# Reordering the expert tiles of a routed feed-forward kernel: five first tiles from the half lists, three experts from the full lists

## The chip, the core and the metric

The kernel runs on one core of a Trainium2 chip. A core has a matmul engine (PE, with its weight loads shown apart as PEld), a vector engine (DVE), a scalar engine (ACT), a general engine (POOL) and a queue engine (SP) that issues DMA transfers; POOL and ACT issue some as well. Each engine works through its own instructions in the order in which they were written, and waits on semaphores for the others. The metric is the device time of one execution in microseconds (us): 1375.17 us before the change, the median of three runs (1374.98 to 1376.15).

## The reference

Two stages. First a causal seven-tap convolution per head, with softmaxed taps (x is 8 x 3584 x 192, so 28,672 tokens of 192 numbers). Then a mixture of eight experts, where tokens are assigned to experts greedily by score under a capacity:

```python
logits = x @ w_gate                       # 28672 x 8
for idx in np.argsort(-logits.flatten()): # best score first
    tok, e = idx // 8, idx % 8
    if assigned[tok] >= 0 or counts[e] >= 3584: continue
    assigned[tok] = e; counts[e] += 1
for e in range(8):
    h = np.maximum(x[assigned == e] @ w1[e], 0.0)   # 192 -> 1024
    out[assigned == e] = h @ w2[e]                  # 1024 -> 192
```

Every expert ends with exactly 3584 tokens, which are seven tiles of 512.

## The kernel before, in words

**Stages.** The convolution runs as matmuls over sixteen blocks and writes its result to a DRAM scratch tensor `attn`; its transposes give the logits on the way. The feed-forward part (class `FFN`) then works through 56 tiles of 512 tokens (eight experts, tiles 0 to 6 each). For a tile the tokens are gathered from `attn` by an index list (POOL, L1206), transposed, multiplied by the first matrix (`l1`, tile `ph`), passed through ReLU, multiplied by the second (`l2`, tile `y`), and scattered to the output by the same list (POOL, L1274). Numbers are kept to full precision by splitting each into a high part and a low part: ACT writes `hh`, the high part of the hidden layer, and DVE writes `hl`, the rest. `run` interleaves, in eight steps f = 0 to 7, the first matrix of tile i with the second matrix of tile i - 1. At the top of tile i it issues the gather of tile i + 2, so the list of tile i + 2 has to be there by then.

**The lists.** Which tokens belong to which expert is worked out while the tiles run. This background work (`Steps`, class `Route`) is a chain of generators: `half(0)` makes lists `ia0` from the first half of the tokens, enough for tile 0 of every expert; `half(1)` makes the full lists `ia` for tiles 0 to 2 (tokens above a safe threshold); `rest` settles the remaining tokens in seven rounds and makes `ib0` (tile 3 of experts 0 to 2); `last` makes `ib` (the remaining tiles). A hook between matmuls takes a few steps of it whenever a planner's running sum says that DVE and ACT are not too far ahead of PE. Where a list is needed and not finished, `drain` writes the remaining steps down at once, with no tile work between them.

**The weights.** The matrices of an expert are also split into high and low parts. The first time an expert comes up, its weights arrive as eight raw pieces (SP, `raw`, four buffers); for each piece `wsplit` lets ACT write the high part and POOL (or DVE, for the two 64-row pieces) the low part (L1187, `w<-raw,w`), has SP store both parts to DRAM scratch (`kw`, `kd`, `kv`; L1190 to L1196), and only then has `wload` issue the raw load of the fourth piece ahead. When the expert comes up again, the split weights are fetched from the scratch in three transfers (`w<-kw`, `dl<-kd`, `w<-kv`), with no splitting. `plan` gives each piece the tile from which it may be handled: four pieces a tile, the first matrix while the tile before the expert's first is running, the second one tile later.

**The order before.** Tile 0 of experts 0 to 7 (tiles numbered 0 to 7 of the run), then tiles 1 and 2 of experts 7 down to 0 (run tiles 8 to 23), then tile 3 of experts 0 to 2, tiles 4 to 6 of experts 2 to 0, and tiles 3 to 6 of experts 3 to 7. So during run tiles 0 to 7 every tile splits eight raw pieces, and all of run tiles 8 to 21 fetch weights that were split before.

Of the kernel before, what the change touches and what calls it, by code (L numbers as in the profile page):

```python
# [10 lines left out]
OP = mybir.AluOpType  # L11
AX = mybir.AxisListType
PSUM = bass.MemoryType.PSUM

NE, D, NTOK, F, CAP = 8, 192, 28672, 1024, 3584
# [278 lines left out]
class Route:  # L294
# [307 lines left out]
    def counts(self, n0):  # L602


        nc, cst, wk = self.nc, self.cst, self.wk
        V, PE = nc.vector, nc.tensor
        n = wk.tile([128, 1], F32, name="k_n")
        self.set = cst.tile([128, 2], F32, name="set")
        V.tensor_scalar(wk.tile([128, G], BF, name="k_b"), self.M1, self.Ts, None, op0=OP.is_ge, op1=OP.add, accum_out=n)
        yield PEW  # L610
        ps = self.bg()
        PE.matmul(ps[:, 24:24 + n0], self.ones, self.tot[0][:, 0:n0], start=True, stop=True, skip_group_check=True)
        for h in range(2):
            PE.matmul(ps[:, 0:8], self.ones, self.tot[h], start=(h == 0), stop=(h == 1), skip_group_check=True)
        for h in range(2):
            PE.matmul(ps[0:8, 8:9], self.tot[h], self.ones[:, 0:1], start=(h == 0), stop=(h == 1), skip_group_check=True)
        PE.matmul(ps[:, 16:17], self.onesf, n, start=True, stop=True, skip_group_check=True)
        self.room = cst.tile([128, 8], F32, name="room")
        self.room8 = cst.tile([8, 1], F32, name="room8")
        b = wk.tile([128, 3], F32, name="k_c")  # L620
        V.tensor_scalar(self.room, ps[:, 0:8], -1.0, float(CAP), op0=OP.mult, op1=OP.add)
        V.tensor_scalar(self.room8, ps[0:8, 8:9], -1.0, float(CAP), op0=OP.mult, op1=OP.add)
        V.tensor_reduce(self.set[:, 1:2], ps[:, 0:8], axis=AX.X, op=OP.add)
        V.tensor_copy(self.set[:, 0:1], ps[:, 16:17])
        V.tensor_reduce(b[:, 2:3], ps[:, 24:24 + n0], axis=AX.X, op=OP.min)
        yield

        V.tensor_reduce(b[:, 0:1], self.room, axis=AX.X, op=OP.max)
        V.tensor_tensor(b[:, 1:2], self.set[:, 0:1], self.set[:, 1:2], op=OP.not_equal)
        V.tensor_scalar(b[:, 2:3], b[:, 2:3], 512.0, None, op0=OP.is_lt)  # L630
        V.tensor_scalar(b[:, 0:1], b[:, 0:1], float(CAP - 128 * TA), None, op0=OP.is_gt)
        V.tensor_reduce(self.bad, b, axis=AX.X, op=OP.max)
        yield
# [451 lines left out]
class FFN:  # L1085
# [47 lines left out]

    def wload(self):
        nc = self.nc
        if self.loaded == len(self.pieces) or self.pieces[self.loaded][3] in ("W1", "W2"):
            return
        _, (e, _), _, what, q = self.pieces[self.loaded]
        t = self.wr.tile([128, 512], F32, name="raw")
        s = slice(512 * q, 512 * q + 512)  # L1140
        if what == "a":
            nc.sync.dma_start(t, self.w1[e, 0:128, s])
        elif what == "d":
            nc.sync.dma_start(t[0:64], self.w1[e, 128:192, s])
            nc.sync.dma_start(t[64:128], self.w1[e, 128:192, s])
        else:
            nc.sync.dma_start(t[:, 0:2 * D].rearrange("p (k d) -> p k d", d=D),
                              self.w2[e, 256 * q:256 * q + 256].rearrange("(k p) d -> p k d", p=128))
        self.RAW[self.loaded] = t
        self.loaded += 1  # L1150
# [198 lines left out]
NL = 3  # L1349


def moe_kernel(ctx, tc, x, weight, wg, w1, w2, out):
    nc = Pace(tc.nc)
    V, P = nc.vector, nc.gpsimd
# [4 lines left out]
    with ExitStack() as cw:  # L1359
# [8 lines left out]
        r = Route(tc, nc, LT, lst, wk, drm)  # L1368
# [5 lines left out]
        ib = lst.tile([128, 8, TB], I32, name="ib")  # L1374
        ib0 = lst.tile([128, NL, 4], I32, name="ib0")

        order = [(e, (0,)) for e in range(NE)]
        order += [(e, (1, 2)) for e in range(NE - 1, -1, -1)]
        order += [(e, (3,)) for e in range(NL)]
        order += [(e, (4, 5, 6)) for e in range(NL - 1, -1, -1)]  # L1380
        order += [(e, (3, 4, 5, 6)) for e in range(NL, NE)]
# [6 lines left out]
        def half(h):  # L1388
            if h == 0:
                yield from r.thresh(0.905)  # L1390
            yield from r.settle(h)
            yield from r.count(r.F, h)
            if h:
                yield from r.counts(NE)
            yield from r.lists(r.F, TA, h, 0 if h else None, *((ia,) if h else (ia0, 8, 4)))

        def rest():
# [47 lines left out]
            k.logits_t(i)  # L1445
            r.top(i)

        def first(e):
            ff.gather(e, [ia0[:, e, b:b + 1] for b in range(4)], NTOK // 2, V)

        def gather():
            if ff.xg and not ff.XG:
# [74 lines left out]

        def idx_of(tile_):
            e, t = tile_[1]
            if t == 0:  # L1530
                return [ia0[:, e, b:b + 1] for b in range(4)]
            if t < 3:
                if len(bg.gens) > 2:
                    bg.drain(2)
                return [ia[:, e, 4 * t + b:4 * t + b + 1] for b in range(4)]
            if t == 3 and e < NL:
                if len(bg.gens) > 1:
                    bg.drain(1)
                return [ib0[:, e, b:b + 1] for b in range(4)]
            if bg.gens:  # L1540
                bg.drain()
            return [ib[:, e, 4 * (t - 3) + b:4 * (t - 3) + b + 1] for b in range(4)]
# [46 lines left out]
```

## Time and profile before

| | |
|---|---|
| median of three runs | 1375.17 us |
| the profiled execution | 1377.14 us, of which the span of its instructions is 1375.2 us |
| mean granted PE clock | 0.964 of full speed |
| first feed-forward matmul | 206 us after the span's start |
| DMA moved | 188.23 MB, 137 GB/s on average |
| weight fetches from scratch | 16 of 1536 KB (first matrix), 16 of 1536 KB (second), 16 of 256 KB |

The profile is one execution. Its page gives the busy time of each engine and the chain of work that ended last; other views of the same trace give each engine's instructions in order of time (with the idle time before an instruction and who ended it), groups of instructions by line and tile, and the busy time of every engine in chosen stretches. A stretch named "run tile 5" here reaches from the first `ph` matmul of that tile to the first of the next; each tile has 40 of them. The PE column of a stretch may be high while PE waits inside its pipeline, so the length of a stretch says more than its busy share.

### The profile page before, as it was taken

Reading aid. Unit: us, or ns where it says so; the run is one execution under the profiler, and the core shown is the slowest. Engines: PE = TensorE matmul, PEld = TensorE weight load, DVE = VectorE, ACT = ScalarE, POOL = GpSimd, SP = SyncE. Lnnn points to the kernel's source line nnn. Section 1 sums busy time; section 2 is a strip of 40 time slices with the busy share of each in tenths; the row PEclk is TensorE's granted clock in tenths of the full one; section 3 lists DMA queues with packets and bytes.
Section 4 is the critical chain, followed back from the end, with each engine's and each line's share of the span. In section 5 each row is a group of like instructions: output and inputs, shape, how many; then the busy total and the mean of one; then the engine's idle time right before and its main releaser. Section 6 shows DMA issues by size and latency. Waiting matters only on the chain.

```text
span 1375.2 us, 20862 instructions
## 1 busy us (share of the span) xinstructions
PE 1288.4 (94%) x7367; PEld 1106.8 (80%) x7367; DVE 1046.1 (76%) x2216; ACT 586.0 (43%) x1242; POOL 637.0 (46%) x607
## 2 busy tenths in 40 slices
PE   5978897998989999999959999999999999999997
PEld 2545564887879989889848999999999999999997
DVE  7598963777988888888877477777777777777772
ACT  4755473447544434434413433333333333333332
POOL 5655566556754443443403344444444444444432
PEclk9998897999999999999959999999999999999999
DMA  9996568677872443343312152324231414141110
GB/s 231 284 271 166 170 218 286 204 231 248 260 260 83 143 137 97 138 143 118 100 60 81 32 197 89 101 89 139 86 99 49 140 44 146 45 142 42 42 35 28
DMA packets 114431, 188.23 MB, mean 137 GB/s; under 512 B 12352, under 2 KB 86544, under 8 KB 110096
## 3 DMA queue, kind: packets, MB, share of 16 engines
q1 hardware_dynamic: 63888, 120.75, 27.6%
q0 software_dynamic: 21504, 44.07, 10.3%
q10 hardware_dynamic: 28928, 22.02, 4.9%
q8 instruction: 59, 0.97, 0.3%
q14 instruction: 52, 0.43, 0.1%
HBM read 114.44 MB, written 72.35 MB: 136 GB/s over the span
## 4 chain that ended last, share of the span: by engine, by line
PE 74%; DVE 14%; DMA 4%; issue 3%; ACT 2%; POOL 2%; SPq 0%; POOLq 0%; DVEq 0%; ACTq 0%
PE ph L53 34%; PE y L53 32%; PE bg L53 4%; DVE X L53 4%; DMA attn<-a 2%; DVE oa L53 2%; DVE aT L53 2%; PE cv L53 1%; DVE hl L53 1%; DMA raw<-in_moe_w_dram 1%; POOL xg L1206 1%; PE pl L53 1%; DVE TH L53 1%; PE pd L53 1%; ACT hi L53 1%
## 5 line engine op out<-in xcount | busy, mean ns | idle before, releaser
L53 PE MATMUL y<-w,hh 128*128 128x384 f32 x1792 | 541.7, 358 | 0.0
L53 ACT ACTIVATE hh<-ph 128x512 fp32r<-128x512 f32 x448 | 267.7, 598 | 508.7 <-PE ph L53 377.6
L53 DVE SCALAR_TENSOR_TENSOR hl<-ph,hh 128x512 fp32r<-128x512 f32 x448 | 308.5, 689 | 196.6 <-ACT hh L53 163.7
L53 PE MATMUL y<-w,hl 128*128 128x192 f32 x1792 | 450.3, 251 | 0.0
L53 PE MATMUL ph<-xa,w 128*128 128x512 f32 x1344 | 401.7, 407 | 17.3 <-DVE hl L53 13.3
L53 PEld LDWEIGHTS y<-w,hl 128*128 128x128 f32 x1792 | 342.8, 191 | 15.4
L53 PEld LDWEIGHTS y<-w,hh 128*128 128x128 f32 x1792 | 338.4, 189 | 17.1
L1274 POOL DMA_INDIRECT out_dram<-yo,ib x128 | 126.9, 992 | 294.9 <-DVE yo L53 279.5
L53 PEld LDWEIGHTS ph<-xa,w 128*128 128x128 f32 x1344 | 221.4, 191 | 42.2 <-DVE hl L53 16.4
L1274 POOL DMA_INDIRECT out_dram<-yo,ia x96 | 107.4, 1118 | 240.6 <-DVE yo L53 202.6
L53 DVE STREAM_TRANSPOSE xs<-xg 32x256 f32<-32x256 f32 x480 | 176.9, 369 | 8.3
L53 PE MATMUL ph<-xd,w 128*128 128x512 f32 x448 | 179.2, 400 | 0.0
L53 PE MATMUL ph<-xd,dl 128*128 128x512 f32 x448 | 176.0, 393 | 0.0
L1206 POOL DMA_INDIRECT xg<-attn,ib x128 | 130.1, 1016 | 70.2 <-issue 69.9
L226 POOL TENSOR_TENSOR lo<-aT,hi 128x768 fp32r<-128x768 f32 x50 | 93.3, 1896 | 73.5 <-ACT hi L53 73.5
L53 PE MATMUL cv<-X,TH 118*128 118x384 f32 x256 | 106.6, 548 | 19.2 <-DVE TH L53 12.8
L1206 POOL DMA_INDIRECT xg<-attn,ia x96 | 105.2, 1096 | 28.8 <-issue 27.6
L53 ACT ACTIVATE yt<-y 128x192 f32<-128x192 f32 x224 | 73.4, 328 | 97.5 <-PE y L53 87.5
L53 DVE TENSOR_TENSOR yo<-y,yt 128x192 f32<-128x192 f32 x224 | 79.6, 355 | 45.6 <-ACT yt L53 42.4
L53 PEld LDWEIGHTS cv<-X,TH 118*128 118x128 f32 x256 | 50.4, 210 | 65.2 <-issue 14.8
L53 PEld LDWEIGHTS ph<-xd,w 128*128 128x128 f32 x448 | 85.2, 190 | 21.3 <-issue 2.2
L53 PEld LDWEIGHTS ph<-xd,dl 128*128 128x128 f32 x448 | 85.1, 190 | 19.9 <-POOL dl L1187 0.3
(241 smaller groups left out, 1233.5 us busy)
## 6 DMA issues: line engine op xcount, KB each, us to landing
w<-kw SPq DMA_DIRECT2D x16, 1536.0 KB
w<-kv SPq DMA_DIRECT2D x16, 1536.0 KB
X<-in_x_dram SPq DMA_DIRECT2D x16, 1344.0 KB
attn<-a ACTq DMA_DIRECT2D x16, 1344.0 KB
kw<-w SPq DMA_DIRECT2D x48, 256.0 KB
kv<-w SPq DMA_DIRECT2D x32, 384.0 KB
raw<-in_moe_w_dram SPq DMA_DIRECT2D x32, 192.0 KB
raw<-in_moe_w_dram SPq DMA_DIRECT2D x16, 256.0 KB
```

Of the source, the lines that this page charges most:

```text
L53: return f(*a, **k)
L226: eng.tensor_tensor(lo, aT, hi.bitcast(F32), op=OP.subtract)
L1206: self.nc.gpsimd.indirect_dma_start(out=t[:, b], out_offset=None, in_=self.attn[0:rows], in_offset=bass.IndirectOffsetOnAxis(ap=idx[b], ax ...
L1274: st = nc.gpsimd.indirect_dma_start(out=self.out, out_offset=bass.IndirectOffsetOnAxis(ap=idx, axis=0), in_=o, in_offset=None, bounds_chec ...
```

## The change

The order of the tiles is written anew. Run tiles 0 to 4 are tile 0 of experts 7, 6, 5, 4 and 3, from the half lists. Then come tiles 1 and 2 of experts 3, 4, 5, 6, 7 (run tiles 5 to 14), and then tiles 0, 1, 2 of experts 2, 1 and 0 (run tiles 15 to 23), all from the full lists. From run tile 24 on the order of tiles is as before. The raw pieces of experts 2, 1 and 0 so come up at run tiles 13 to 19, behind four fetches from the scratch; `wload` now steps over fetches to find the next raw piece. The weights are fetched from scratch 13 times in place of 16. The check that the half lists are long enough looks at experts 3 to 7 alone.

```diff
-        PE.matmul(ps[:, 24:24 + n0], self.ones, self.tot[0][:, 0:n0], ...)
+        PE.matmul(ps[:, 24:32 - n0], self.ones, self.tot[0][:, n0:8], ...)
...
     def wload(self):
         nc = self.nc
-        if self.loaded == len(self.pieces) or self.pieces[self.loaded][3] in ("W1", "W2"):
+        while self.loaded < len(self.pieces) and self.pieces[self.loaded][3] in ("W1", "W2"):
+            self.loaded += 1
+        if self.loaded == len(self.pieces):
             return
...
-        order = [(e, (0,)) for e in range(NE)]
-        order += [(e, (1, 2)) for e in range(NE - 1, -1, -1)]
+        order = [(e, (0,)) for e in range(NE - 1, NL - 1, -1)]
+        order += [(e, (1, 2)) for e in range(NL, NE)]
+        order += [(e, (0, 1, 2)) for e in range(NL - 1, -1, -1)]
         order += [(e, (3,)) for e in range(NL)]
...
-                yield from r.counts(NE)
+                yield from r.counts(NL)
...
-            if t == 0:
+            if t == 0 and e >= NL:
                 return [ia0[:, e, b:b + 1] for b in range(4)]
             if t < 3:
                 if len(bg.gens) > 2:
                     bg.drain(2)
```

(`NE` is 8 and `NL` is 3.) The first run tile from the full lists is now number 5 in place of 8, so its gather stands at the top of run tile 3 in place of 6, and the last steps of `half(1)` are drained there. At the top of run tile 22 the drain that finishes `ib0` stands in both kernels.

**DVE at the top of run tile 3** (`oa` is a one-hot block of the list sort, `asm` the sorted list, `m_f` to `ia` the arithmetic that makes token numbers of it, `hl` and `yo` tile work). Before:

```order
L53 TENSOR_TENSOR oa<-irep,q 128x1024
L53 TENSOR_TENSOR dl<-raw,w_2604 64x512
L53 SCALAR_TENSOR_TENSOR hl<-ph,hh 128x512 x2
L53 TENSOR_TENSOR yo<-y,yt 128x192
L53 SCALAR_TENSOR_TENSOR hl<-ph,hh 128x512
L53 TENSOR_TENSOR asm<-asm,bg 128x192
L53 TENSOR_SCALAR m_f<-asm 128x96
```

With the change:

```order
L53 TENSOR_TENSOR oa<-irep,q 128x1024
L53 TENSOR_TENSOR dl<-raw,w_2604 64x512
L53 TENSOR_TENSOR asm<-asm,bg 128x192
L53 TENSOR_SCALAR m_f<-asm 128x96
L53 TENSOR_SCALAR off<-bad 128x1
```

The three `hl` of run tile 3 that lay between the sort and the list now come after the list.

**POOL in run tiles 4 and 5, and in 13 and 14** (`w<-raw,w` are the low parts of a raw piece, `xg` a gather, `out_dram` a scatter). Before, from the gather at the top of run tile 4 on, and so on to run tile 7:

```order
L1206 DMA xg<-attn,ia_105 128x192 x4
L1187 TENSOR_TENSOR w_3138<-raw,w_3138 128x2x192
L1274 DMA out_dram<-yo,ia_105 28672x192
L1187 TENSOR_TENSOR w_3138<-raw,w_3138 128x2x192 x2
L1274 DMA out_dram<-yo,ia_105 28672x192
L1187 TENSOR_TENSOR w_3138<-raw,w_3138 128x2x192
L1187 TENSOR_TENSOR w_3267<-raw,w_3267 128x512
L1274 DMA out_dram<-yo,ia_105 28672x192
L1187 TENSOR_TENSOR w_3267<-raw,w_3267 128x512
L1274 DMA out_dram<-yo,ia_105 28672x192
```

With the change the last split of the first phase stands in run tile 4; from run tile 13 on:

```order
L1208 DMA xg<-attn,ia 128x192 x4
L1189 TENSOR_TENSOR w_5319<-raw,w_5319 128x512
L1276 DMA out_dram<-yo,ia 28672x192
L1189 TENSOR_TENSOR w_5319<-raw,w_5319 128x512
L1276 DMA out_dram<-yo,ia 28672x192 x3
L1208 DMA xg<-attn,ia 128x192 x4
L1189 TENSOR_TENSOR w_5572<-raw,w_5572 128x2x192
L1276 DMA out_dram<-yo,ia 28672x192
L1189 TENSOR_TENSOR w_5572<-raw,w_5572 128x2x192 x2
L1276 DMA out_dram<-yo,ia 28672x192
L1189 TENSOR_TENSOR w_5572<-raw,w_5572 128x2x192
L1276 DMA out_dram<-yo,ia 28672x192 x2
```

The second half of run tile 4 and run tiles 5 to 7 lose 18 splits in all; run tiles 13 to 16, 18 and 19 get 2 or 4 each, 20 in all (for expert 0 POOL also takes the two 64-row pieces).

**DVE before the drain at run tile 22** (`X` and `c_mu` are the last pass over the scores, `F` the final assignment that the count on PE needs). Before, `F` is written in the drain, with no `hl` behind it:

```order
L53 TENSOR_TENSOR X_7539<-X_7423,c_mu 128x512
L53 TENSOR_TENSOR yo<-y,yt 128x192
L53 TENSOR_TENSOR X_7539<-X_7423,c_mu 128x512
L53 TENSOR_TENSOR X_7539<-X_7424,c_mu 128x512 x2
L53 SCALAR_TENSOR_TENSOR F<-X_7539,F 128x1024 x2
L53 TENSOR_SCALAR k_b,u_c<-c_mu 128x256
```

With the change:

```order
L53 SCALAR_TENSOR_TENSOR hl<-ph,hh 128x512
L53 SCALAR_TENSOR_TENSOR F<-X_7406,F 128x1024
L53 TENSOR_TENSOR yo<-y,yt 128x192
L53 SCALAR_TENSOR_TENSOR F<-X_7406,F 128x1024
L53 SCALAR_TENSOR_TENSOR hl<-ph,hh 128x512
L53 TENSOR_TENSOR xa<-pa,xa 128x512
L53 SCALAR_TENSOR_TENSOR hl<-ph,hh 128x512
```

`F` is now written inside run tile 21, with `hl` of that tile behind it.

More of the change, by code (lines that the diff above doesn't have):

```diff
@@ L611, in counts @@
         ps = self.bg()
-        PE.matmul(ps[:, 24:24 + n0], self.ones, self.tot[0][:, 0:n0], start=True, stop=True, skip_group_check=True)
+        PE.matmul(ps[:, 24:32 - n0], self.ones, self.tot[0][:, n0:8], start=True, stop=True, skip_group_check=True)
         for h in range(2):
@@ L624, in counts @@
         V.tensor_copy(self.set[:, 0:1], ps[:, 16:17])
-        V.tensor_reduce(b[:, 2:3], ps[:, 24:24 + n0], axis=AX.X, op=OP.min)
+        V.tensor_reduce(b[:, 2:3], ps[:, 24:32 - n0], axis=AX.X, op=OP.min)
         yield
@@ L1446, in end, with first @@
             r.top(i)
-        def first(e):
-            ff.gather(e, [ia0[:, e, b:b + 1] for b in range(4)], NTOK // 2, V)
+        def first(i):
+            e = tiles[i][1][0]
+            ff.gather(i, [ia0[:, e, b:b + 1] for b in range(4)], NTOK // 2, V)
         def gather():
```

## The prediction

> **What bounds the kernel now.** I read the page first, for the engine that carries the chain that ended last.
>
> ```profile
> PE 1288.4 (94%) x7367; PEld 1106.8 (80%) x7367; DVE 1046.1 (76%) x2216; ACT 586.0 (43%) x1242; POOL 637.0 (46%) x607
> PE 74%; DVE 14%; DMA 4%; issue 3%; ACT 2%; POOL 2%; SPq 0%; POOLq 0%; DVEq 0%; ACTq 0%
> ```
>
> PE is the bound, but a quarter of the chain is others' work. To see where, I cut the feed-forward part into stretches, one a run tile where the change acts. Columns: stretch, length, busy us (and instructions) of PE, PEld, DVE, ACT, POOL, then the granted clock, the DMA share and GB/s.
>
> ```profile
> 292.90:318.30 25.40, 22.62 (x163) 20.03 (x162) 17.69 (x34) 13.23 (x25) 14.29 (x13) 1.00 0.57 184
> 318.30:340.20 21.90, 19.99 (x115) 17.52 (x114) 12.03 (x19) 19.22 (x54) 15.14 (x15) 1.00 0.80 258
> 340.20:363.30 23.10, 20.45 (x114) 18.19 (x113) 22.79 (x36) 12.86 (x30) 16.70 (x16) 0.96 0.90 296
> 363.30:383.30 20.00, 20.00 (x115) 18.07 (x114) 17.45 (x39) 11.28 (x28) 14.70 (x14) 0.96 0.77 239
> 383.30:410.50 27.20, 22.58 (x121) 19.55 (x119) 23.60 (x56) 10.38 (x21) 13.57 (x13) 0.87 0.74 263
> 410.50:668.40 257.90, 256.85 (x1512) 230.68 (x1511) 220.10 (x522) 113.04 (x278) 113.72 (x104) 1.00 0.36 120
> 668.40:720.60 52.20, 37.48 (x325) 32.89 (x324) 41.55 (x107) 12.48 (x24) 9.39 (x9) 0.73 0.25 83
> 772.10:1340.20 568.10, 568.10 (x3235) 515.64 (x3234) 425.63 (x915) 215.52 (x434) 244.85 (x244) 1.00 0.27 91
> ```
>
> The first five rows are run tiles 3 to 7, the sixth is tiles 8 to 20 (13 of them, 257.9/13 = 19.84 each), the seventh tile 21 with the drain behind it, the last tiles 24 to 54 (31, 18.33 each). A tile alone costs 18.3; with rounds of background work beside it 19.8, PE never idle for more than 1.05 in 13 tiles, though every second tile fetches split weights there: fetches cost nothing, at a DMA share of 0.36. But tiles 4 to 7, which split raw pieces beside the same rounds, cost 21.9 + 23.1 + 20.0 + 27.2 = 92.2.
>
> Why: two causes. The first is in the chain of waits of tile 4 (start us, us, what).
>
> ```profile
> 331.11 1.03 POOL w L1187
> 332.16 0.32 SPq L1190
> ...
> 334.40 4.30 DMA raw<-in_moe_w_dram
> 338.72 0.55 ACT w L53
> 339.27 0.58 ACT hh L53
> ```
>
> A raw load is issued only after POOL's split and the store behind it; ACT waits for it, with `hh` queued behind, and PE waits for that. The second is in the order of time of DVE, POOL and PE in tiles 5 and 7, with one undisturbed row of tile 8:
>
> ```profile
> 350.83 2.71 DVE L53 SCALAR_TENSOR_TENSOR c_mu<-X 128x256 f32<-128x256 f32 x1
> 351.25 2.00 POOL L1187 TENSOR_TENSOR w<-raw,w 128x384 fp32r<-128x384 f32 x2
> 394.47 2.74 DVE L53 TENSOR_SCALAR r_dd<-r_d 128x8 f32<-128x8 f32 x1
> 395.19 1.98 POOL L1187 TENSOR_TENSOR w<-raw,w 128x384 fp32r<-128x384 f32 x2
> 360.12 0.96 PE L53 MATMUL ph<-xa,w 128*128 128x512 f32 x3 [1.79 <-DVE hl L53]
> 399.70 1.65 PE L53 MATMUL ph<-xa,w 128*128 128x512 f32 x3 [3.01 <-DVE hl L53]
> 424.27 0.41 DVE L53 SCALAR_TENSOR_TENSOR c_mu<-X 128x256 f32<-128x256 f32 x1
> ```
>
> While POOL does a pair of splits, a DVE instruction of 0.41 takes 2.71: it ends when the pair ends. `hl` is late, `ph` is not freed, PE idles 1.79 and 3.01, and behind it the clock drops (0.96 and 0.87 in those stretches).
>
> **The change part by part.** *A: run tiles 4 to 7 lose their splits.* They should cost what tiles 8 to 20 do: 4 x 19.84 = 79.4, so 12.8 less. Tile 4 keeps the four pieces of expert 3, but the late load in its chain is a piece of the next expert and goes. I take -12; bounds -9 (tile 4 keeps its 21.9 and tile 7 two of its 7.4 too many) and -13.
>
> *B: the drain at the top of run tile 3.* The rows for it are the same end of a list in the drain at tile 22 (chain of waits), and, in the order of time of PE and POOL and in the chain of waits, where the pieces stand now in tile 3:
>
> ```profile
> 715.41 0.61 ACT X L53
> 716.02 0.05 issue
> 716.06 1.09 PE bg L53 x8
> 717.17 1.95 ACT X L53 x2
> 719.12 0.04 issue
> 719.17 1.68 PE bg L53 x17
> 294.66 1.15 PE L53 MATMUL bg<-X,oa 128*128 128x16 bf16 x16
> 298.01 1.22 PE L53 MATMUL bg<-identb,X 128*128 128x128 bf16 x16
> 295.63 1.04 POOL L1206 DMA_INDIRECT xg<-attn,ia  x1 [0.30 <-issue]
> 304.49 1.03 POOL w L1187
> 305.54 0.32 SPq L1190
> 305.91 2.71 DMA raw<-in_moe_w_dram
> ```
>
> The last 16 sort matmuls (1.15), ACT's copy (0.61), half the transposes (1.22/2), two copies (1.95) and the last matmuls (of the 1.68 some 0.4 belong to the list) follow each other with nothing beside them: 1.15 + 0.61 + 0.61 + 1.95 + 0.4, with the small gaps about 5 us. Of it some 3 (1.15 + 1.22 + 0.7) is PE work that tile 3 does anyway, so 2 is new. Behind it: 13 small DVE instructions make the list, and `hl` of f = 0 waits for them; POOL's gather for tile 5, at 295.63 now, waits for the list (the drain's 5 and some 2.5 for the 13, counted from 292.9), about 5 later, and behind it stand the scatter of tile 2, four splits, the stores on SP and the raw loads that ACT waits for: the last three rows are on the chain, with no slack. PE is 2 later itself, so up to 3 more can surface; and a clock window can be lost:
>
> ```profile
> 360.00:365.00 5.00, 4.88 (x17) 4.36 (x18) 4.94 (x7) 1.97 (x6) 2.47 (x2) 0.66 0.95 297
> ```
>
> 0.34 of 5 us, 1.7, after an idle spell of 1.79. I take +4; bounds +2 (the drain alone) and +8 (2 + 3 and the clock lost twice).
>
> *C: the splits of experts 2, 1 and 0 in run tiles 13 to 16, 18 and 19.* Nothing is removed here: POOL does 20 splits in place of 18, at the mean of this group (all of the run):
>
> ```profile
> L1187 POOL TENSOR_TENSOR w<-raw,w 128x384 fp32r<-128x384 f32 (+1 forms) x48 | 52.9, 1118 | 13.4 <-ACT w L53 12.6
> ```
>
> But there are four pieces a tile, not eight, so 2 or 4 splits beside DVE's 17 us a tile in place of 6, the first four raws were loaded nine tiles before, and DMA has room. Tile 6 is the row for splits that cost nothing: six of them, 20.0. Tile 5 is the row for splits that meet the pass over the scores (`X`, `c_mu`): 3.3 over. By the order, tiles 15 and 18 have that pass beside their splits, with half the splits or a little more; the others mostly have the largest-value search and small steps, as tile 6. I take +2 for each of those two tiles, +4. Bounds 0 and +11 (all the excess of tiles 5 and 7, 3.3 + 7.4, comes back).
>
> [...]
>
> *D: the drain at tile 22.* Now PE waits in it first for `F`:
>
> ```profile
> 693.66 0.26 PE L53 MATMUL bg<-ones,F 128*128 128x1 bf16 x4 [4.67 <-DVE F L53]
> 694.80 0.48 PE L53 MATMUL bg<-ones,F 128*128 128x1 bf16 x12 [0.87 <-DVE F L53]
> ```
>
> With the change `F` and the steps before it lie in tile 21, under its matmuls: 4.67 + 0.87 = 5.5 less, of which I take -5. Bound -3: in tile 21 DVE ends late, as its share of that tile grows. What is late next is the place and sort behind `F`, which is the same.
>
> *At nothing:* three fetches less (their cover is the DMA's 0.64 idle share; tiles 8 to 20 show PE waiting for none), the matmul over five columns in place of eight, and other experts in the first tiles (same sizes).
>
> Sum: -12 + 4 + 4 - 5 = -9. The span 1375.2 becomes 1366.2; the profiled execution took 1377.14, 1.9 more than its span, and the median lies 2.0 below that execution, so the forecast is 1375.17 - 9 = 1366.
>
> **The rivals.** *The lock moves with the splits.* C is +11: -12 + 4 + 11 - 5 = -2, 1373. For it: as many splits, beside as many rounds. Against: half as many a tile, and `ph` has two buffers, so DVE may be about 2 us late (a step is 2.3) before PE notices.
>
> *Slower: every split tile becomes a tile 5.* DVE has 220.1 of 257.9 filled in tiles 8 to 20, 2.9 free a tile; from the point where a tile's blocked time passes that and the 2 of the buffers, PE idles and the clock drops with it. Six tiles at 3.3 are +20: -12 + 4 + 20 - 5 = +7, 1382. Against: four splits are at most 4.5 us of POOL, and only the part that meets a blocked kind counts.
>
> *All the excess goes.* B costs its 2, C nothing, A -13, D -5.5: -16.5, 1359. For it: tile 6. Against: the raw load on the chain of tile 3.
>
> **How the numbers follow.** 0.62 for the forecast, 0.15 for the lock that moves, 0.09 for slower, 0.14 for all the excess. A change under 0.2% (2.75 us) can't be told from none. The forecast's own range (-5 to -14) and the last rival lie below 1372.4: 0.76 faster. The lock that moves gives the 0.14 within 0.2% and a little of the 0.10 slower. The range 1358 to 1376 takes in the last rival and the lock that moves, and leaves out the slower case.
>
> **What would show it.** A: tiles 4 to 7 near 19.8 each, no ACT wait for a raw load there, `c_mu` back at 0.4 in the first round. B: tile 3 some 4 longer than 25.4, PE waiting for ACT's `X` before it. C: tiles 13 to 19 at 20 to 22, long `X` beside `w<-raw,w` in 15 and 18. D: no 4.67 before the count, the drain stretch 52.2 about 5 shorter. It would be wrong if tiles 13 to 19 lost clock, or if the tiles 4 to 7 stayed above 21 with no split beside them: then the first round, not the splits, was their cause.

## The result, and the profile after

The changed kernel takes **1368.72 us**, the median of four runs (1367.05 to 1370.40), beside 1375.66 for the kernel before on the same chip (1374.98 to 1376.98): a ratio of **0.9949**, 95% interval 0.9934 to 0.9963. The forecast was 1366 with a range of 1358 to 1376. The later runs were made on other chips, where the kernel before itself takes up to 1379.05, so they are compared by ratios.

The page of the changed kernel, its busy times and its chain of work (span 1368.5 us):

```profile
PE 1287.0 (94%) x7367; PEld 1104.3 (81%) x7367; DVE 1054.3 (77%) x2214; ACT 588.5 (43%) x1242; POOL 636.7 (47%) x609
PE 77%; DVE 13%; DMA 3%; ACT 2%; issue 2%; POOL 1%; SPq 0%; POOLq 0%; ACTq 0%
```

PE has 77% of the chain in place of 74%; DVE was busy 8 us longer (1054.3 against 1046.1) with two instructions less. To see where, the feed-forward part is cut into stretches again. First the kernel before: run tiles 2 and 3 together, 4 to 7, and 14 to 19 (stretch, length, busy us and instructions of PE, PEld, DVE, ACT, POOL, then granted clock, DMA share, GB/s):

```profile
261.77:318.34 56.57, 51.48 (x389) 46.00 (x388) 46.02 (x80) 25.84 (x50) 33.57 (x28) 0.97 0.64 208
318.34:410.47 92.13, 82.96 (x456) 73.25 (x455) 75.80 (x147) 53.73 (x133) 60.07 (x56) 0.94 0.80 265
528.58:649.22 120.64, 120.07 (x709) 107.37 (x708) 101.40 (x253) 50.15 (x120) 52.01 (x48) 1.00 0.38 125
```

The same with the change, and as a fourth row run tile 21 with the drain behind it (52.20 before):

```profile
263.80:322.45 58.65, 54.03 (x389) 48.34 (x388) 45.59 (x82) 29.17 (x64) 34.60 (x29) 0.91 0.62 194
322.45:402.01 79.56, 78.46 (x458) 70.15 (x457) 67.30 (x159) 38.84 (x97) 38.23 (x37) 1.00 0.53 170
519.60:647.00 127.40, 121.70 (x706) 107.05 (x704) 118.55 (x244) 58.52 (x136) 70.48 (x66) 1.00 0.41 132
667.59:712.34 44.75, 35.20 (x316) 31.31 (x315) 35.55 (x84) 12.47 (x24) 10.55 (x9) 0.76 0.27 93
```

| stage | before | after | difference | forecast |
|---|---|---|---|---|
| A: run tiles 4 to 7, no splits from 5 on | 92.1 | 79.6 | -12.6 | -12 |
| B: run tiles 2 and 3, early drain | 56.6 | 58.7 | +2.1 | +4 |
| run tiles 8 to 13 | 118.1 | 117.6 | -0.5 | 0 |
| C: run tiles 14 to 19, late splits | 120.6 | 127.4 | +6.8 | +4 |
| run tile 20 | 19.2 | 20.6 | +1.4 | 0 |
| D: run tile 21 and the drain | 52.2 | 44.8 | -7.4 | -5 |
| sum of these | | | -10.3 | -9 |

(The differences are taken from the unrounded lengths.) The spans differ by 6.7 only. The other 3.6 lie where nothing was changed: the first feed-forward matmul 1.6 later, run tiles 0 and 1 0.4 longer, the last stage 1.6 longer, all of it after the last scatter is issued. These places scatter between executions of one kernel: over all profiles of this study the first matmul falls between 202.4 and 208.0, and the last stage takes 34.8 to 36.8.

**Where C comes from** shows best in run tile 16. Its stretch (columns as above), and then in the order of time its DVE, POOL and PE (start us, us, engine, line, operation, tiles, count, and the idle time before with who ended it):

```profile
561.25:584.98 23.73, 20.33 (x119) 17.77 (x118) 21.96 (x45) 9.91 (x22) 12.09 (x12) 1.00 0.45 147
```

```profile
569.22 1.61 DVE L53 TENSOR_SCALAR r_x<-r_x 128x8 f32<-128x8 f32 x2
571.41 2.72 DVE L53 TENSOR_TENSOR X<-j,r_dd 128x120 f32<-128x120 f32 x1
574.24 0.28 DVE L53 TENSOR_TENSOR X<-j,r_dd 128x120 f32<-128x120 f32 x1
571.99 1.99 POOL L1189 TENSOR_TENSOR w<-raw,w 128x384 fp32r<-128x384 f32 x2
575.18 0.95 PE L53 MATMUL ph<-xa,w 128*128 128x512 f32 x3 [0.97 <-DVE hl L53]
580.25 0.21 PE L53 MATMUL bg<-r_cc,ones 128*128 128x120 bf16 x1 [1.84 <-DVE r_cc L53]
```

An instruction on 120 numbers a partition takes 2.72 where its twin takes 0.28: it ends as POOL's pair of splits ends (571.99 + 1.99 = 573.98). `hl` stands behind it, `ph` is not freed, and PE waits 0.97. This is tile 5 of before over again, in a stage where the forecast expected it elsewhere. The longer wait of the tile, 1.84, is the same on another way: a matmul of the background work stands between those of the tile and needs `r_cc`, and DVE comes to `r_cc` late because the pair of `X` ahead of it takes 1.90 beside POOL's next split. With a third wait of 0.58 at the tile's end these are its 3.4 us of idle PE.

**The drain at run tile 22.** The last second-matrix matmul of tile 21, and the first instruction behind the count of `F`, before (order of time of PE and DVE):

```profile
688.75 0.25 PE L53 MATMUL y<-w,hl 128*128 128x192 f32 x1
697.07 0.69 DVE L53 SCALAR_TENSOR_TENSOR X<-bg,F 128x512 f32<-128x512 f32 x1 [0.18 <-PE bg L53]
```

and with the change, with the wait of PE that comes first in the drain now:

```profile
687.88 0.25 PE L53 MATMUL y<-w,hl 128*128 128x192 f32 x1
689.08 1.28 DVE L53 SCALAR_TENSOR_TENSOR X<-bg,F 128x512 f32<-128x512 f32 x2
696.00 4.89 PE L53 MATMUL bg<-X,oa 128*128 128x16 bf16 x64 [6.83 <-DVE oa L53]
```

From the one to the other were 8.1 us (697.07 - 689.00), and are 0.95. The wait for `F` is gone as forecast, and the sums behind the count, up to that instruction, now run almost wholly under tile 21's matmuls too.

**The early drain.** PE in the order of time at the top of run tile 3, and the stretch behind it:

```profile
296.52 0.67 PE L53 MATMUL bg<-X,oa 128*128 128x16 bf16 x8 [0.86 <-DVE oa L53]
297.88 1.46 PE L53 MATMUL bg<-identb,X 128*128 128x128 bf16 x16 [0.69 <-ACT X L53]
299.71 0.32 PE L53 MATMUL bg<-iq,ones 128*128 128x192 bf16 x1 [0.36 <-ACT X L53]
300.62 0.39 PE L53 MATMUL bg<-c_oh,X 128*128 128x24 bf16 x8 [0.39 <-ACT X L53]
```

```profile
298.60:305.50 6.90, 6.15 (x39) 5.39 (x38) 4.35 (x16) 2.95 (x4) 0.83 (x1) 0.51 0.15 35
```

Four waits, 2.3 us in all, and then 6.9 us at a mean clock of 0.51.

### The profile page after: what moved, and what is told of

Read it like the earlier page. It is cut to its first block, busy times and chain, and to the rows that moved or that the text cites. A ratio compares the mean times of both kernels' runs of the same rounds, so it can differ in the third digit from the quotient of the medians.

```text
span 1368.5 us, 20850 instructions
## 1 busy us (share of the span) xinstructions
PE 1287.0 (94%) x7367; PEld 1104.3 (81%) x7367; DVE 1054.3 (77%) x2214; ACT 588.5 (43%) x1242; POOL 636.7 (47%) x609
## 3 DMA queue, kind: packets, MB, share of 16 engines
q0 software_dynamic: 21504, 44.07, 10.6%
## 4 chain that ended last, share of the span: by engine, by line
PE 77%; DVE 13%; DMA 3%; ACT 2%; issue 2%; POOL 1%; SPq 0%; POOLq 0%; ACTq 0%
PE ph L53 36%; PE y L53 34%; DVE X L53 4%; PE bg L53 4%; DMA attn<-a 2%; DVE aT L53 2%; DVE oa L53 2%; PE cv L53 2%; DVE hl L53 1%; PE pl L53 1%; DVE TH L53 1%; POOL xg L1208 1%; PE pa L53 1%; PE pd L53 1%; ACT hi L53 1%
## 5 line engine op out<-in xcount | busy, mean ns | idle before, releaser
L53 PEld LDWEIGHTS ph<-xa,w 128*128 128x128 f32 x1344 | 221.1, 191 | 37.1 <-DVE hl L53 12.9
L1276 POOL DMA_INDIRECT out_dram<-yo,ia x96 | 102.5, 1068 | 229.8 <-DVE yo L53 188.6
L1208 POOL DMA_INDIRECT xg<-attn,ia x96 | 108.3, 1128 | 35.9 <-issue 33.1
L53 PEld LDWEIGHTS ph<-xd,dl 128*128 128x128 f32 x448 | 85.1, 190 | 19.8 <-POOL dl L1189 0.3
```

The lines of the kernel that those rows point to most:

```text
L53: return f(*a, **k)
L1208: self.nc.gpsimd.indirect_dma_start(out=t[:, b], out_offset=None, in_=self.attn[0:rows], in_offset=bass.IndirectOffsetOnAxis(ap=idx[b], ax ...
L1276: st = nc.gpsimd.indirect_dma_start(out=self.out, out_offset=bass.IndirectOffsetOnAxis(ap=idx, axis=0), in_=o, in_offset=None, bounds_chec ...
```

## The experiments

Theory: the late splits cost what they cost because POOL's subtraction blocks DVE (the lock), and D comes from background work that is put ahead, whatever the order of the tiles. Rivals: C is late raw loads or ACT's share of the splits; D belongs to the new order; the three fetches saved are part of the gain. Ratios are to the kernel before on the same chip, with 95% intervals.

### The changed kernel again

No edit.

> The changed kernel once more, for a second profile and a time on this chip beside the others. If the stages of its first profile are the kernel's own and not one execution's, tiles 2 and 3 come to 58 to 60 us, 4 to 7 to 79 to 80, 14 to 19 to 126 to 128 and the stretch of tile 21 to 44 to 46 again, and the first feed-forward matmul (207.6 us in the first profile, 206.0 before, with the same instructions ahead of it) lies anywhere between 202 and 208. The ratio to the kernel before is 0.993 to 0.997.

Measured: 1369.88 us, ratio **0.9936** [0.9923, 0.9949]. The stages of the table repeat the first profile within 0.2, but for run tiles 14 to 19 (128.8 against 127.4), where the clock was at half for 3.4 us in tile 16. (Outside of the table run tiles 0 and 1 and run tile 22 are 0.6 and 0.7 shorter, the first matmul is 0.4 later.) The two intervals together put the change at -5.1 to -10.6 us of 1375, with the forecast's -9 in them.

### Late low parts filled with zeros

```diff
-        eng.tensor_tensor(lo, r[0:n], hi[0:n].bitcast(F32), op=OP.subtract)
+        if self.done >= 40 and eng is self.nc.gpsimd:
+            eng.memset(lo.bitcast(F32), 0.0)
+        else:
+            eng.tensor_tensor(lo, r[0:n], hi[0:n].bitcast(F32), op=OP.subtract)
```

The low parts that POOL makes for experts 2, 1 and 0 are left out (zeros); POOL's instruction then has no input (`MEMSET w<-` below).

> The changed kernel, but in run tiles 13 to 19 POOL sets the low parts of the weights to zero in place of subtracting (so this part of the computation is left out; the raw loads, the high parts on ACT, the stores and the order of every other instruction stay). Theory, the lock: what tiles 14 to 19 cost over the kernel before (127.3 against 120.7 us in the two profiles, +6.6) comes from DVE instructions that stand still while POOL reads SBUF in a split (19.5 us of stretched DVE instructions there). A zero fill reads nothing, so the stretched instructions go and these six tiles come back to 119 to 121.5, the whole to about 6 us under the changed kernel (1362 to 1364). Rival, raw loads and ACT: the late raws, their ACT copies and stores cost it; they are all still there, so tiles 14 to 19 stay at 126 to 128 and the time at 1368 to 1369.

Measured: 1359.11 us, **0.9866** [0.9849, 0.9884]. Run tiles 14 to 19, and POOL's fill in tile 16 in the order of time:

```profile
516.06:637.01 120.95, 119.86 (x706) 106.85 (x704) 103.42 (x246) 58.53 (x136) 58.70 (x66) 1.00 0.43 140
```

```profile
566.00 0.82 POOL L1190 MEMSET w<- 128x384 f32 x2
```

The stage falls from 127.40 to 120.95, near the 120.64 of the kernel before, with the raw loads, ACT's part and the stores all in place: the rival falls. The time fell by more than the stage, 0.7% to 0.8% against the 0.5% that 6.4 of 1375 are: in this profile the first feed-forward matmul comes 3.9 earlier, 203.6 for 207.6, where nothing was edited, so the stage carries the argument and not the time. (A fill is also shorter, 0.41 a piece, so POOL is free sooner; what speaks for the lock and not for that is DVE.) DVE is busy 15 us less (103.42 for 118.55) for the same work. Which of its instructions had been stretched is in the groups of DVE over run tiles 13 to 20 (line, engine, operation, tiles, shapes, count | busy us, mean ns of one | idle before). The changed kernel:

```profile
L53 DVE SCALAR_TENSOR_TENSOR hl<-ph,hh 128x512 fp32r<-128x512 f32 x65 | 44.4, 684 | 9.7 <-ACT hh L53 9.2
L53 DVE SCALAR_TENSOR_TENSOR X<-LT,c_T 128x256 f32<-128x256 f32 x28 | 15.1, 591 | 0.1
L53 DVE MAX8 r_w<-X 128x8 f32<-128x256 f32 x32 | 11.5, 412 | 0.0
L53 DVE TENSOR_TENSOR X<-j,r_dd 128x120 f32<-128x120 f32 x4 | 3.6, 892 | 0.1
```

and with the zeros:

```profile
L53 DVE SCALAR_TENSOR_TENSOR hl<-ph,hh 128x512 fp32r<-128x512 f32 x65 | 44.6, 688 | 17.6 <-ACT hh L53 15.9 <-issue 1.0
L53 DVE SCALAR_TENSOR_TENSOR X<-LT,c_T 128x256 f32<-128x256 f32 x28 | 11.9, 480 | 0.1
L53 DVE MAX8 r_w<-X 128x8 f32<-128x256 f32 x32 | 11.5, 414 | 0.0
L53 DVE TENSOR_TENSOR X<-j,r_dd 128x120 f32<-128x120 f32 x4 | 1.1, 284 | 0.1
```

`hl` (one input from PSUM) and `MAX8` (one input) are the same in both, 684 and 688 ns, 412 and 414. Of these four groups the two that read two tensors from SBUF are stretched: one of the four `TENSOR_TENSOR` (by 2.4) and two of the 28 `X<-LT,c_T` (by 0.7 and 2.4). With the fill, which reads nothing, their means are 284 and 480 ns.

### The same in the kernel before

The same edit in the kernel before (the low parts of POOL from run tile 4's second half to 7 are left out).

> The kernel before, but with the same zero fill on POOL for the raw pieces of experts 5 to 7 (second half of run tile 4 to first half of run tile 7; the low parts of their weights are so left out). Theory, the lock: tiles 5 and 7 lose their excess (3.3 + 7.4 over 19.84), c_mu is back at 0.4 us; tile 4 keeps the 2 us of its late raw load; the time falls by 8 to 11 us. Rival, DMA: tiles 4 to 7 are slow for their DMA share of 0.74 to 0.90 and the raw loads that ACT waits for; loads and stores are unchanged, so they stay at 88 to 92 together and the time falls by 0 to 3 us.

Measured: 1367.05 us, **0.9925** [0.9905, 0.9944]. Run tiles 4 to 7:

```profile
314.84:396.61 81.77, 78.76 (x456) 70.08 (x455) 65.49 (x147) 53.90 (x134) 47.73 (x56) 1.00 0.88 295
```

92.13 becomes 81.77, and the clock 1.00: 10.4 of the 12.6 of A go with the lock, though all raw loads stay and DMA is at a share of 0.88. The other 2.2 are in tile 4, which keeps its 21.9, and tile 7, 21.4.

### The early drain alone

```diff
 # the kernel before, at the top of a run tile
+            if i == 3:
+                bg.drain(2)
```

> The kernel before, with the one edit that the full lists are drained at the top of run tile 3, as in the changed kernel; the order of tiles and the splits stay as before. Theory: the drain costs 2 to 3 us at tiles 2 and 3 together (56.5 before), and puts all later background work ahead, so that 50 steps in place of 60 are left for the drain at tile 22 and the stretch of tile 21 with it falls from 52.2 to about 45 (as in the changed kernel, 44.8); in sum -4 to -5 us. Rival: the shorter drain at tile 22 comes from the order of tiles (fewer splits on DVE and ACT before it); then the stretch of tile 21 stays at 50 to 52 and the time rises by 2 to 4 us.

Measured: 1372.98 us, **0.9955** [0.9939, 0.9971]. Run tiles 4 to 7, and tile 21 with its drain:

```profile
320.18:411.99 91.81, 83.25 (x459) 72.53 (x457) 77.64 (x160) 49.83 (x121) 60.09 (x55) 0.96 0.81 268
670.78:715.40 44.62, 34.92 (x317) 31.24 (x315) 34.22 (x80) 12.37 (x24) 9.66 (x9) 0.78 0.29 97
```

In the old order, two lines give all of D (44.62) and all of B (run tiles 2 and 3 take 58.7), and the 1.3 of tile 20, while A stays at 91.81. B, D and tile 20 are therefore one thing: the eleven steps that are written down early leave fewer for the end. The new order itself is A and C, -12.6 and +6.8 by the stages. By the times alone it can't be told from the early drain: the interval here, 0.9939 to 0.9971, overlaps with both of the changed kernel.

### Six first tiles in place of five

```diff
-        order = [(e, (0,)) for e in range(NE - 1, NL - 1, -1)]
+        order = [(e, (0,)) for e in range(NE - 1, NF - 1, -1)]    # NF = 2; the other uses of NL here too
```

> Six experts' first tiles from the half lists in place of five (7 to 2), then tiles 1 and 2 of these, then tiles 0 to 2 of the other two. The full list is then first needed at the top of run tile 4, where it is ready, so nothing is drained at tile 3; 55 steps are left for the drain at tile 22 (60 before, 51 with the change). Theory: tiles 2 and 3 as before the change (56 to 57), tiles 4 and 5 keep splits and cost 21 to 23 each, 6 and 7 19.3 to 20; 14 to 19 with 14 POOL splits in place of 20 about 124; the stretch of tile 21 48 to 50. In sum 2 to 4 us over the changed kernel, ratio 0.996 to 0.999 to the kernel before. Rival: the early drain is a pure loss, and without it the kernel is 2 us faster than the changed one.

Measured: 1368.80 us, **0.9932** [0.9920, 0.9944], as the changed kernel and so between the two expectations. No list is due at tile 3, so nothing is drained there. Run tiles 2 and 3:

```profile
263.28:319.71 56.43, 51.40 (x389) 45.96 (x388) 46.05 (x80) 25.84 (x50) 33.58 (x28) 0.97 0.65 207
```

B is back to nothing (56.43 for 58.65, the clock at 0.97 again), but one more expert is split early (run tiles 4 to 7 at 82.5, 2.9 more) and the last drain has more left (tile 21 at 46.7, 1.9 more). Fewer late splits give 4.5 back in run tiles 14 to 19 (122.9). By these stages some 2 us are won, which the runs can't tell from the changed kernel.

### Late pieces spread over the tile

```diff
-                if i < n:
+                if i < n and (self.done < 40 or f % 2 == 0 or ...):   # late raw pieces at even f only
```

> The changed kernel, with the late raw pieces split at every second step of a tile (f = 0, 2, 4, 6) in place of four steps in a row; nothing is left out. Theory, the lock: as many DVE instructions can be stretched (15 to 20 us in sum), but two buffers of the hidden layer cover one stretch of up to about 2 us at a time, so fewer reach PE: tiles 14 to 19 fall from 127.3 to about 123, the time by 2 to 4 us. Rival: what counts is the sum of the stretched time, which DVE has no room for: tiles 14 to 19 stay at 126 to 128 and the time within 1 us of the changed kernel.

Measured: 1364.61 us, **0.9897** [0.9881, 0.9912]. Run tiles 14 to 19:

```profile
519.52:642.59 123.07, 120.61 (x705) 107.12 (x704) 112.89 (x244) 57.96 (x136) 69.68 (x66) 1.00 0.42 136
```

DVE is still stretched (112.89; with zeros 103.42), but less, and the pieces stand further apart: 127.40 becomes 123.07.

### Spread, and the late low parts on DVE

```diff
+        if self.done >= 40:
+            eng = self.nc.nc.vector        # not counted by the planner
         eng.tensor_tensor(lo, r[0:n], hi[0:n].bitcast(F32), op=OP.subtract)
```

On top of the spread pieces; everything is computed.

> The changed kernel with the late pieces split at every second step, and with all their low parts on DVE in place of POOL (not counted by the planner, so that the background work isn't held back). Theory, the lock: POOL has nothing to do that blocks DVE, so the 15.8 us of stretched DVE instructions that the spread kernel still shows in tiles 13 to 20 go, and about 13 us of DVE work of its own (20 pieces at 0.65) comes in their place, in small pieces: tiles 14 to 19 at 121 to 123, the drain at tile 22 has 45 steps in place of 51 and its stretch falls to 42 or 43; 2 to 4 us faster than the spread kernel. Rival: DVE is full, and its own work costs PE as much as the standing still does: tiles 14 to 19 stay at 123 to 126.

Measured: **1359.35 us, 0.9854** [0.9840, 0.9869], the best of the study. Run tiles 14 to 19 and tile 21, one of the moved instructions in DVE's order of time, and PE's first wait in the drain:

```profile
519.26:640.16 120.90, 120.04 (x705) 106.99 (x704) 113.08 (x271) 61.46 (x152) 56.86 (x48) 1.00 0.43 140
661.33:703.08 41.75, 34.90 (x317) 31.08 (x315) 32.53 (x78) 12.47 (x24) 10.35 (x9) 0.81 0.28 100
```

```profile
562.78 0.53 DVE L1191 TENSOR_TENSOR w<-raw,w 128x384 fp32r<-128x384 f32 x1
686.72 4.88 PE L53 MATMUL bg<-X,oa 128*128 128x16 bf16 x64 [4.11 <-DVE oa L53]
```

DVE does a low part in 0.53 where POOL takes 1.0 and holds DVE up meanwhile: with 18 more low parts in these six tiles DVE is busy 113.08, less than the 118.55 of the changed kernel, and the stage comes to the 120.95 of the zeros with nothing left out. Less of the end is left for the drain too (41.75; the first wait 4.11 for 6.83).

### The same once more

> The spread kernel with the late low parts on DVE once more, unchanged, on another chip or another turn. It asks whether its ratio of 0.9854 holds, and whether the 0.9891 of the kernel that also moved the low parts of run tiles 3 and 4 to DVE was the edit or the chip. Theory, that the edit did that: the ratio is again 0.984 to 0.987. Rival, that chips and executions scatter by that much in places that the edit does not touch (the waits at tiles 0 and 2, the clock at tile 23, the last transfer): the ratio is 0.987 to 0.990.

Measured, on another chip: 1356.40 us, **0.9862** [0.9845, 0.9878]. It holds.

### Four first tiles

```diff
+NF = 4          # for NL in the order, the counts and the choice of list; late from piece 32 on
+                # on top of the spread pieces
```

> Four experts' first tiles in place of five, then tiles 1 and 2 of these, then tiles 0 to 2 of the other four, with the late pieces split at every second step. The full list is needed at the top of run tile 2: 44 steps of it are drained there in place of 11 at tile 3, and 22 in place of 51 are left for the drain at tile 22. Theory: a step drained early is a step less to drain late, and the early ones (sorting, where PE, DVE and ACT work together) cost PE less than the late ones: tiles 1 to 3 lose 8 to 14 us, the stretch of tile 21 falls to 30 to 36, tiles 14 to 19 (32 late pieces in tiles 10 to 20) at 122 to 125; the time 2 to 8 us under the spread kernel with five. Rival: a step costs the same wherever it is drained: what tile 21 gains, tiles 1 to 3 lose, and the time is within 2 us of the spread kernel with five or above it.

Measured: 1369.08 us, **0.9920** [0.9901, 0.9939]. Run tiles 0 and 1, 2 and 3, and 8 to 13:

```profile
206.58:282.84 76.26, 60.31 (x389) 46.46 (x389) 44.25 (x92) 27.56 (x52) 33.30 (x31) 0.79 0.66 219
282.84:325.20 42.36, 41.22 (x230) 36.60 (x227) 30.05 (x58) 27.23 (x71) 27.20 (x25) 0.95 0.68 221
403.53:528.07 124.54, 121.30 (x699) 107.76 (x698) 112.55 (x257) 57.06 (x132) 64.72 (x60) 0.99 0.44 146
```

The full lists are now drained at the top of run tile 2. Against the changed kernel that costs 20.1 in tiles 0 and 1, gives back 16.3 in tiles 2 and 3 and 8.7 at tile 21 (36.0), and eight more late pieces cost 6.9 in tiles 8 to 13. Here draining more of it earlier wins nothing, as the rival had it.

### Fetches issued twice

```diff
+            for _ in range(2):
                 self.nc.sync.dma_start(W.bitcast(F32), self.kept1[e])
                 ...                     # the same for dl<-kd and w<-kv
```

> The changed kernel with each of its fetches of split weights from the scratch issued twice (13 more of 1536, 256 and 1536 KB, 43 MB more in all; the second copy writes the same bytes). Theory, that fetches cost nothing where DMA has room: run tiles 5 to 12 and 24 to 54 stay where they are (tiles 8 to 13 at 117.6, tiles 25 to 54 at 548.8, each within 0.5), and the time against the kernel before is that of the changed kernel, 0.993 to 0.995. Rival, that the three fetches saved were part of the gain: 13 more cost what three saved times four, so that tiles 5 to 12 and 24 to 54 grow by 1 us or more per doubled fetch, the raw loads of tiles 13 to 19 come later, and the ratio is 1.00 or above.

Measured: 1373.82 us, **0.9964** [0.9952, 0.9976], which neither side expected. Run tiles 5 to 12 and 25 to 54, where nearly all the fetches are, in the changed kernel and then with each issued twice:

```profile
343.33:499.99 156.66, 156.66 (x922) 141.06 (x921) 139.06 (x334) 68.24 (x164) 67.64 (x64) 1.00 0.39 128
783.06:1331.86 548.80, 548.80 (x3122) 498.13 (x3121) 421.23 (x901) 211.01 (x420) 236.28 (x236) 1.00 0.28 93
```

```profile
342.22:499.48 157.26, 157.25 (x922) 141.30 (x921) 138.75 (x334) 67.84 (x164) 67.50 (x64) 1.00 0.62 214
786.34:1335.32 548.98, 548.98 (x3122) 498.17 (x3121) 416.89 (x901) 206.92 (x420) 236.82 (x236) 1.00 0.42 142
```

There 12 doubled fetches cost 0.8 together, and the rival's 1 us each falls; the 13th is in run tiles 20 and 21, which stay at 20.5 and 44.8. Against the second profile of the changed kernel 2.5 of the 2.8 us that the span is longer are in run tiles 22 to 24, where none is issued (the clock: 1.1 in tile 22, where the half speed of the drain lasts longer, and 1.4 in tile 23, below). The ratio is 0.15% and 0.28% above the two of the changed kernel; whether the extra traffic makes such a loss of clock likelier, or the chip does, stays open.

### DVE from run tile 3 on

```diff
-        if self.done >= 40:
+        if self.done >= 28:
```

On top of the spread kernel with late low parts on DVE.

> The spread kernel with the late low parts on DVE, and with those of run tiles 3 and 4 (from the 29th piece on) on DVE too, so that POOL splits nothing beyond tile 2. Theory, that what is left over 19.8 in tile 4 is blocked DVE time and a late raw load behind POOL: the long DVE instructions of tiles 3 and 4 go, tile 4 comes from 21 to 20 or 20.5, and the time is 0 to 1.5 us below that kernel's 0.9854 of the kernel before (0.984 to 0.9855). Rival, that DVE becomes the bound where eight pieces fall in one tile: DVE takes some 6 us more in tiles 3 and 4, hl comes late, and tiles 3 and 4 together are 2 us or more longer (0.987 or above).

Measured: 1364.25 us, **0.9891** [0.9871, 0.9910]. Run tiles 3 and 4, here and then in the second run of the kernel it is made from:

```profile
301.19:323.10 21.91, 21.91 (x119) 19.58 (x115) 17.44 (x37) 13.84 (x37) 7.83 (x7) 0.88 0.56 176
323.10:343.54 20.44, 19.72 (x115) 17.44 (x113) 14.53 (x32) 12.96 (x35) 8.63 (x8) 1.00 0.92 305
```

```profile
298.12:319.70 21.58, 21.58 (x118) 19.38 (x115) 15.72 (x32) 13.19 (x34) 14.29 (x13) 0.89 0.51 162
319.70:340.62 20.92, 19.79 (x115) 17.37 (x113) 14.33 (x27) 14.05 (x39) 13.08 (x13) 1.00 0.89 281
```

Tile 4 gains 0.5 as expected, tile 3 loses 0.3: nothing is won. The time is in the rival's range, but not by the rival's cause, since tiles 3 and 4 together are 42.4 for 42.5. The 0.3% that it is slower lie elsewhere in its profile (the first matmul 2.5 later, tile 2 at 38.3 for 37.1 with 6.8 us at half the clock ahead of the drain for 3.4, run tiles 8 to 20 2.6 longer in all, tiles 22 and 23 2.0, the last stage 1.8), none of it where the edit acts. The unedited kernel was not run on that chip, so the edit isn't shown to be slower.

### The old order with both cures

```diff
 # the kernel before
+            if i == 3:
+                bg.drain(2)
...
+        if self.done >= 40:
+            eng = self.nc.nc.vector
```

> The kernel before, in its own order of tiles, with the drain at the top of run tile 3 and the low parts of its last 24 pieces (run tiles 4 to 7) on DVE in place of POOL. It asks whether the new order is needed at all. Theory, that the order is needed to spread the pieces: there is no lock, but eight pieces a tile put some 6 us more on DVE in each of tiles 5 to 7, which leaves it no room, so that tiles 4 to 7 come to 84 to 88 (92.1 before, 79.6 with the change), and the time lies between the early drain alone (0.9955) and the spread kernel with low parts on DVE (0.9854), near 0.990. Rival, that the order did nothing which the other two edits do not do: tiles 4 to 7 come to 80 to 82 and the ratio to 0.985 to 0.987.

Measured: 1365.64 us, **0.9908** [0.9887, 0.9928], where the theory put it. Run tiles 4 to 7:

```profile
319.95:408.21 88.26, 82.02 (x458) 71.70 (x457) 78.26 (x182) 49.86 (x121) 41.91 (x37) 0.98 0.85 277
```

With the low parts of these pieces off POOL the old order still pays 88.3, 8.7 over the changed kernel's 79.6, with DVE at 78.26 for 67.30 and DMA at 0.85 for 0.53. The zeros in the old order, above, tell the two apart: there the stage took 81.77 at a DMA share of 0.88, with DVE at 65.49. So 6.5 of the 8.7 come with the work on DVE, and 2.2 stay with the pieces themselves. The new order is worth having (0.9908 against 0.9854 and 0.9862), because with four pieces a tile in place of eight DVE has room for them (run tiles 14 to 19 above, 120.90).

## Why the prediction was right, point by point

**The sum** was -9; the changed stages give -10.3 in the profile, and the runs -6.9 and -8.9. That it came out so near is in part luck: two terms were too kind (C, and tile 20 at nothing) and two too hard (B and D), and they cancel.

**A** (-12) was right at -12.6, and the first of its causes is shown: the zeros in the kernel before give the lock 10.4. They leave 2.2 to what else the pieces cost; the late load in tile 4 is likely a part of it, but no run takes that out alone. Tile 4 came to 20.9, not 19.8, by two waits of PE for `hl`, 0.57 and 0.53: ahead of the first DVE waits 1.3 before a split of its own (`dl`), ahead of the second one of the last splits stretches an `X` by 2.4.

**B** (+4) measured +2.1. Step that failed: "up to 3 more can surface" by the late gather. The gather of run tile 5 did come late: 3.8 us after tile 3's first matmul (304.67 - 300.86), where the forecast's row had it 2.7 after, and that matmul itself comes behind the drain. But nothing of it reached PE, which is busy for all of the 21.59 of run tile 3, where it had idled 2.8 of 25.40 before. PE's idle time in tiles 2 and 3 did not grow at all (56.57 - 51.48 = 5.1 before, 58.65 - 54.03 = 4.6 after). The whole price is the clock: 0.91 for 0.97 over 58 us, and PE busy 54.03 for 51.48 with the same number of matmuls. Six first tiles, without the drain, have the 56.4 and the 0.97 of before.

**C** (+4) measured +6.8, the term that was mis-sized most, and its tiles were the wrong ones. "Tiles 15 and 18 ... +2 each; the others mostly have the largest-value search and small steps, as tile 6": against 19.84 tiles 15 and 18 came to +0.6 and -0.3, while 14, 16 and 19, which have the search, came to +1.4, +3.9 and +2.3. The search itself (`MAX8`) is not blocked (412 ns, with zeros 414), but the small two-input steps between its matmuls are (1.41 us for 0.17 of `r_no<-r_no,r_dd` in tile 14, 2.72 for 0.28 of `X<-j,r_dd` in tile 16), and they lie on the way to `hl` and to the matmuls of the background work. Tile 6 of before, at 20.0, was no rule: its splits met `MAX8` (at most 0.43 us), `MATCH_REPLACE8` (0.41) and instructions with one input from PSUM (`hl` 0.67 and 0.69, `xd` 0.69, `yo` 0.35), and none of these is longer than usual. The zeros (127.40 to 120.95) show that all of C but 0.3 is the lock.

**D** (-5) measured -7.4. "What is late next is the place and sort behind `F`, which is the same" held: from `X<-bg,F` to the first matmul of run tile 22 it is 23.5 us before (720.60 - 697.07) and 23.3 with the change (712.34 - 689.08). Mis-sized is the term ahead of it. The forecast counted PE's two waits for `F`, 5.5, and left out the sums between the count and the place, which run under tile 21's matmuls as well now: the 8.1 us from the last matmul to `X<-bg,F` became 0.95, 7.1 less. And the cause was not the order but the early drain, which the prediction had counted as a cost only: in the old order it gives the same 44.6. The +1.4 of tile 20 is the other side of it, background work put ahead.

**Fetches at nothing** held where they are issued (0.8 for 12 doubled).

**The rivals.** "The lock moves with the splits" was right about the mechanism, and more than that: DVE time over the usual length of the same instructions, beside a split, adds up to 10.1 us in run tiles 4 to 7 before (7 instructions) and to 18.4 in run tiles 14 to 19 with the change (13 instructions). Of these 20 instructions 17 read two tensors from SBUF, and three (`c_T`, `r_dd`, `r_x`) one. But PE paid 10.4 for the 10.1, and 6.4 (127.40 - 120.95) for the 18.4, so the time was the forecast's and not 1373. Of the 10.4 some 4.2 was lost clock (PE busy 82.96, with zeros 78.76, the clock 0.94 and 1.00). In run tiles 14 to 19 of the first profile the clock is 1.00; in the second it fell in tile 16, and PE paid 7.8 for 17.4 (128.78 - 120.95). That pieces which stand closer together cost more is borne out by the spread ones, where 13.0 blocked us cost 2.1 (123.07 - 120.95); between the old place and the new one the work beside the pieces differs too. DVE is no emptier in the new place: without the blocked time it fills 65.7 of the 79.6 us that run tiles 4 to 7 should take, and 100 of 121 in 14 to 19. As many splits did block as much DVE time as before and more, but the +11, which takes PE's old price for it, was too high: C came to +6.8. "Every split tile becomes a tile 5" happened in one of six: in tile 16 DVE has 21.96 of 23.73 filled and PE idles 3.4. "All the excess goes" was reached only by taking the low parts off POOL: 0.9854 and 0.9862 of the kernel before, 1355 to 1356 by the 1375.17.

## What to carry to other kernels

A DVE instruction that POOL holds up looks like a long instruction, not like a wait (here 2.72 us in place of 0.28): compare each with the median of its own kind, see what POOL does at that moment, and price the blocked time by how closely the blocked pieces stand together (here 1.0 us of PE for each blocked us with eight pieces a tile, 0.35 to 0.45 with two or four, 0.16 with those spread out). Moving such work to another place did not lower the blocked time (10.1 us before, 18.4 after); spreading it lowered its price, and giving it to the engine that it was blocking removed it here, at 0.53 in place of 1.0 each. Background work with a late due date is worth putting ahead only as far as tiles have room for it, and the gain shows far behind the edit.

## What the runs showed of the hardware

**Which instructions are blocked** is in the groups above: a mean of 892 for 284 ns of a 128x120 `TENSOR_TENSOR`, 591 for 480 of `X<-LT,c_T`, nothing for `hl` and `MAX8`. A small `TENSOR_SCALAR` on one tensor was hit as well (`r_x`, 1.61 for a pair; 0.21 undisturbed in the kernel before). Beside a fill no two-input instruction is longer, but such a `TENSOR_SCALAR` is: in each of the two runs with zeros one `r_dd<-r_d` takes 0.33 or 0.35 in place of 0.17 and ends with the fill. (Longer there are also the two `r_x` of tile 16 and the `r_tl` behind them; they end at 566.1, as POOL's issue of a scatter does at 566.0.)

**The clock falls in pieces of 3.4 us, and not in every execution.** Two profiles of the spread kernel with low parts on DVE, run tiles 22 to 24, first run and second:

```profile
703.08:776.10 73.02, 72.38 (x511) 64.98 (x509) 43.92 (x95) 25.02 (x47) 24.25 (x23) 0.95 0.11 34
```

```profile
699.61:770.29 70.68, 70.04 (x512) 62.94 (x509) 43.97 (x95) 25.14 (x47) 23.89 (x23) 0.98 0.12 35
```

The same instructions and the same single wait of 0.64 (the difference of length and PE's busy time), 2.3 us apart, 1.5 of it in tile 23. In the first, the clock falls there after that wait, which ends at 730.21:

```profile
731.00:734.60 3.60, 3.60 (x15) 3.12 (x15) 1.85 (x5) 0.60 (x1) 2.99 (x3) 0.53 0.29 85
```

Of the 14 profiles of this study six show that piece and eight do not, in both orders of tiles. The 3.60 us at 0.53 here and the 6.90 at 0.51 above are some 3.4 and 6.8 at half speed, and 0.64 of waiting among small matmuls is all that PE idled in the 3 us ahead of the piece here.

Which executions lose the piece can be told from the clock in the traces. In each of the 14 all changes of the granted clock lie on one grid of 3.41 us, which starts elsewhere in each execution. In the six the wait of 0.64 begins 1.8 to 2.4 us behind a point of the grid (in the profile above at 729.57, the piece at 731.19); in the eight it begins 2.5 to 3.3 us, or 0.1, behind one (2.5 in the kernel before and in the changed one). The same wait so costs nothing or 1.5 us by where it happens to fall. That such waits make up much of the 3 us by which runs of one kernel differ here is the author's estimate; no run shows it.
